# A decode block that records its own instructions and writes its own waits, in place of a scheduling context

## The chip, the cores and the metric

One core of one Trainium2 chip runs the kernel. The metric is device time in microseconds (us) of one execution. The engines are TensorE (PE, its weight loads PEld), VectorE (DVE), ScalarE (ACT), GpSimd (POOL) and SyncE (SP), which here issues every DMA. Each engine works through its own queue of instructions in order; engines and DMAs are tied together by semaphores only.

## What is computed

One decode step for 4 tokens of width 448: layer norm, attention with 16 query heads over 8 heads of cached keys and values (the last 1024 positions of 4096), an output projection with a residual, then two layer norms and a two-layer MLP with a GELU, and a second residual.

```python
def _A_ref(x, k_cache, v_cache, wq, wo):          # B, Sq, D = 4, 1, 448
    Hq, Dh = 16, 256
    Hkv, Sk = k_cache.shape[1], k_cache.shape[2]  # 8, 4096
    W = min(4096, max(256, Sk // 4))              # 1024
    rep = Hq // Hkv
    q = (x @ wq).reshape(B, Sq, Hq, Dh).transpose(0, 2, 1, 3)
    k = jnp.repeat(k_cache[:, :, Sk - W:, :], rep, axis=1)
    v = jnp.repeat(v_cache[:, :, Sk - W:, :], rep, axis=1)
    p = _softmax(jnp.einsum("bhqd,bhkd->bhqk", q, k) * (Dh ** -0.5), axis=-1)
    o = jnp.einsum("bhqk,bhkd->bhqd", p, v)
    return o.transpose(0, 2, 1, 3).reshape(B, Sq, Hq * Dh) @ wo

def _B_ref(x, w1, b1, w2, b2):                    # F = 1792
    y = _layernorm(x, axis=-1)
    h = _gelu(jnp.einsum("bsd,df->bsf", y, w1) + b1)
    return jnp.einsum("bsf,fd->bsd", h, w2) + b2

x = A_x
h = x + _A_ref(_layernorm(x, axis=-1), A_k_cache, A_v_cache, A_wq, A_wo)
h2 = h + _B_ref(_layernorm(h, axis=-1), B_w1, B_b1, B_w2, B_b2)
```

All of it is float32, and nearly all of the bytes are the cached keys and values and the weights, each read once.

## The kernel before

**Loads.** The host lays the inputs out so that each DMA fills 128 partitions with long rows. On the chip a ring of three slots (`slot`, 15872 columns of float32 each) takes them in turn, all issued by SyncE in the order of the program (`load`, line 58, and line 285 for two small ones): `t0` (first query weights and the token, then the first keys), `l1` to `l8` (keys, values and projection weights, 6 or 8 MB each), and last the slots `te0`, `te1` and `te2`, which are filled in pieces: keys `k7`, values with output weights `vo`, values `v7` in two pieces, output weights `wo`, then `w1` in two pieces and `w2` in four. A load into a slot waits until the slot's former contents have been read. Three loads ahead of the computation are thus under way or queued.

**Computation.** The eight heads of keys and values are taken in pairs, each pair giving one tile `n` of 0 to 3. `project` and `queries` make the queries (tile `qT`), `scores` (line 184) multiplies them with the keys, `softmax` (lines 187 to 205) takes the maximum on VectorE and the exponential on ScalarE, `transpose_p` (line 212) turns the probabilities on PE and copies them to `pT` on VectorE (line 218), `values` (line 226) multiplies with the values into `po`, `transposed_output` scales by the reciprocal of the sums (`rec`, lines 203 and 204; line 243) and transposes, and `add_output` (line 257) adds the projection to `acc`. Between tiles PE runs matmuls on a zeroed bfloat16 tile `idle` (`keep_warm`, line 269), whose results nothing reads.

**Head.** While the first loads come, the constants are made: `ident` by GpSimd, `sel` and `fold` from it by VectorE (lines 97 to 114), zeroed tiles by memsets. Then the first layer norm (lines 288 to 296) gives `yT`, and three copies spread token and biases over `wide` (lines 301 to 306). The reciprocal root is a power taken on GpSimd (`rsqrt`, line 148).

**Tail.** After the last values: residual and sums (line 464), two mean subtractions, variances, `w1` (`pu`, line 501), GELU (line 508), then `w2`: its first 8 chunks into `pa` (line 528), which ScalarE copies (`pas`), the other 6 into `py` (line 539) together with `pas`. `hb` (line 482) is the residual with a bias; `res` (line 545) adds it to `py`, and line 546 stores `res`, 64 KB.

**Order and waits.** The body runs inside a scheduling context (`tile.TileContext`, line 619). Tiles come from its pools, it finds which instructions depend on each other, sets the semaphores and waits, and places the tiles. With `manual_schedule` the queues of PE, SP and ACT keep the order of the program; those of VectorE and GpSimd are ordered by the context. At the context's end stand instructions of its own, which carry line 619 in the profile. Those of line 614 are the setup of the program object.

Of the kernel before, what the change touches and what calls it, by code (L numbers as in the profile page):

```python
# [1 line left out]

# [5 lines left out]

F32 = mybir.dt.float32
BF16 = mybir.dt.bfloat16  # L10
AF = mybir.ActivationFunctionType
ALU = mybir.AluOpType
AX = mybir.AxisListType
PSUM = bass.MemoryType.PSUM

B, D = 4, 448
HQ, HKV, SK, DH = 16, 8, 4096, 256
# [3 lines left out]
P = 128  # L21
# [9 lines left out]
SLOT = CACHE + 2 * WEIGHTS + HALF  # L31
# [1 line left out]
EPS = 1e-5  # L33
SCALE = DH ** -0.5

@with_exitstack
def block_kernel(ctx: ExitStack, tc, wq0, k0, wq1, l1, l2, l3, l4, l5, l6, l7, l8, k7, vo, v7, wo, w1, w2, out):
    nc = tc.nc
    const = ctx.enter_context(tc.tile_pool(name="const", bufs=1))
    ring = ctx.enter_context(tc.tile_pool(name="ring", bufs=3))  # L40
    work = ctx.enter_context(tc.tile_pool(name="work", bufs=2))
    once = ctx.enter_context(tc.tile_pool(name="once", bufs=1))
    ps_s = ctx.enter_context(tc.tile_pool(name="ps_s", bufs=2, space=PSUM))
    ps_t = ctx.enter_context(tc.tile_pool(name="ps_t", bufs=2, space=PSUM))
    ps_o = ctx.enter_context(tc.tile_pool(name="ps_o", bufs=1, space=PSUM))
    ps_m = ctx.enter_context(tc.tile_pool(name="ps_m", bufs=2, space=PSUM))
    ps_w = ctx.enter_context(tc.tile_pool(name="ps_w", bufs=1, space=PSUM))

    def slot(name):
        return ring.tile([P, SLOT], F32, tag="r", name=name)

    def load(t, at, src, pieces=None):
        dst = t[:, at : at + src.shape[-1]]
        at = 0
        for n in pieces or (src.shape[-1],):
            nc.sync.dma_start(dst[:, at : at + n], src[:, at : at + n])  # L58
            at += n
        return dst  # L60

    def cut(t, sizes):
        parts, at = [], 0
        for n in sizes:
            parts.append(t[:, at : at + n])
            at += n
        return parts
# [11 lines left out]
    def keys(t):  # L79
        return t.rearrange("p (c b k) -> p c b k", c=2, b=B)  # L80
# [7 lines left out]


    ident = const.tile([P, P], F32, name="ident")  # L90
    make_identity(nc, ident)
    mhalf = const.tile([P, B], F32, name="mhalf")
    nc.vector.memset(mhalf, -0.5)
    mean = const.tile([P, P], F32, name="mean")
# [83 lines left out]
    def score_tiles(n):  # L178
        return [ps_s.tile([P, 512], F32, tag="s", name=f"s{n}_{h}") for h in range(2)]

    def scores(s, g, h, kt):
        for c in range(2):
            for b in range(B):
                nc.tensor.matmul(  # L184
                    s[h][b * Q : (b + 1) * Q, :], qT[g][:, c, b, :], kt[:, c, b, :],
                    start=(g == 0 and c == 0), stop=(g == 1 and c == 1),
                )

    def softmax(n, s):
        mx = work.tile([P, 2], F32, tag="mx", name=f"mx{n}")  # L190
        for h in range(2):
            nc.vector.reduce_max(mx[:, h : h + 1], s[h], axis=AX.X)  # L192
        nm = work.tile([P, 1], F32, tag="nm", name=f"nm{n}")
        nc.vector.tensor_scalar(nm, mx[:, 0:1], mx[:, 1:2], -SCALE, op0=ALU.max, op1=ALU.mult)  # L194
        p = once.tile([P, 2 * 512], F32, tag="p", name=f"p{n}")
        sums = work.tile([P, 2], F32, tag="sums", name=f"sums{n}")
        for h in range(2):
            nc.scalar.activation(  # L198
                p[:, h * 512 : (h + 1) * 512], s[h], AF.Exp, bias=nm, scale=SCALE,
                accum_out=sums[:, h : h + 1],  # L200
            )
        rec = work.tile([P, 1], F32, tag="rec", name=f"rec{n}")
        nc.vector.tensor_add(rec, sums[:, 0:1], sums[:, 1:2])
        nc.vector.reciprocal(rec, rec)
        return p, rec

    def transpose_p(n, p):
        pts = []
        for h in range(2):
            pt = ps_t.tile([P, 4, P], F32, tag="t", name=f"ppt{n}_{h}")  # L210
            for c in range(4):
                nc.tensor.transpose(pt[:, c, :], p[:, (4 * h + c) * P : (4 * h + c + 1) * P], ident)  # L212
            pts.append(pt.rearrange("p (c i) (b q) -> p c i b q", i=2, b=B))
        for g in range(2):
            for h, src in enumerate(pts):
                for i in range(2):
                    at = (2 * g + i) * REP
                    nc.vector.tensor_copy(
                        pT[g][:, 2 * h : 2 * h + 2, :, at : at + REP],
                        src[:, :, i, :, 2 * g * REP : (2 * g + 1) * REP],  # L220
                    )

    def values(g, vt, po, pairs=range(NKC // 2), alone=False):
        for c in pairs:
            for b in range(B):
                nc.tensor.matmul(  # L226
                    po[b * Q : (b + 1) * Q], pT[g][:, c, b, :], vt[c][:, :, b, :],
                    start=(c == 0 and (alone or g == 0)), stop=(c == NKC // 2 - 1 and (alone or g == 1)),
                )
# [5 lines left out]
    def columns(t, j):  # L235
        if j < 3:
            return t[:, j * P : (j + 1) * P].rearrange("p (i c) -> p i c", i=2)
        return t[:, None, 3 * P :].to_broadcast([t.shape[0], 2, H])
# [32 lines left out]
    def keep_warm_between():  # L271
        warm = ps_t.tile([P, 512], F32, tag="t", name="between")
        keep_warm(6, warm)

    def po_tile(g, pool=ps_o, tag="o"):
        return pool.tile([P, 2, DH], F32, tag=tag, name=f"po{g}")


    t = slot("t0")
    wqt, xT, b2T, b1T = cut(load(t, 0, wq0), (WEIGHTS, ND * B, 4, 4 * 4))  # L280
    wqt = wq_parts(yT[0], wqt)
# [25 lines left out]
    for at, n in ((0, 2), (2 * P, 4)):  # L307
# [3 lines left out]
        cols = min(n * P, rs.shape[1] - at)  # L311
# [4 lines left out]
    s = score_tiles(0)  # L316
# [3 lines left out]
    def both_queries(n, wqs):  # L320
        pq = pq_tile(n)
        for g in range(2):
            project(pq, wq_parts(yT[g], wqs[g]), g == 0)
        queries(n, pq)

    def outputs(n, po, rec, wos):
        transposed_output(n, po, rec, range(2))
        for g in range(2):
            add_output(n, g, output_weights(wos[g]))

    ka, kb, va = cut(load(slot("l1"), 0, l1), (HALF, HALF, HALF))
    for h, kt in enumerate((ka, kb)):
        scores(s, 1, h, keys(kt))
    p, rec = softmax(0, s)
    transpose_p(0, p)
    po = po_tile(0)
    values(0, chunks(va), po, range(0, 2))
    keep_warm_between()

    vb, v, wo_a, wo_b = cut(load(slot("l2"), 0, l2), (HALF, CACHE, WEIGHTS, WEIGHTS))  # L340
# [7 lines left out]
    s = score_tiles(1)  # L348
# [4 lines left out]

    k2, v, wq_a, wq_b = cut(load(slot("l4"), 0, l4), (HALF, CACHE, WEIGHTS, WEIGHTS))
    scores(s, 1, 1, keys(k2))
    p, rec = softmax(1, s)
    both_queries(2, (wq_a, wq_b))
    transpose_p(1, p)
    po = po_tile(1)
    values(0, chunks(v), po)  # L360
    keep_warm_between()

    v, wo_a, wo_b, ka = cut(load(slot("l5"), 0, l5), (CACHE, WEIGHTS, WEIGHTS, HALF))
    values(1, chunks(v), po)
    s = score_tiles(2)
# [5 lines left out]
    scores(s, 0, 1, keys(kb))  # L371
    for h, kt in enumerate((ka, k2)):
        scores(s, 1, h, keys(kt))
    p, rec = softmax(2, s)
    transpose_p(2, p)
    keep_warm_between()

    v, va, wq_a, wq_b = cut(load(slot("l7"), 0, l7), (CACHE, HALF, WEIGHTS, WEIGHTS))
# [8 lines left out]
    s = score_tiles(3)  # L387
# [7 lines left out]
    v, wot = cut(load(e[1], 0, vo), (CACHE, 2 * D))  # L395
# [6 lines left out]
    w2t = cut(load(e[2], CACHE, w2, (8 * D, 3 * D, 2 * D, D)), NFC * (D,))  # L402
    for h in range(2):
        scores(s, 1, h, kt[h])
    p, rec = softmax(3, s)


    warm0 = ps_o.tile([P, 512], F32, tag="o", name="warm0")
# [1 line left out]
    def fill(n):  # L410
        for _ in range(n):
            nc.tensor.matmul(warm0[:Q], yT[0][:, 0, :], kt[0][:, 0, 0, :], start=True, stop=True)

    fill(2)
    transpose_p(3, p)
    fill(3)
    po = po_tile(3)
    values(0, vt, po, alone=True)
# [27 lines left out]
    def w1_part(a, j):  # L446
        if a < 3:
            return slice(0, P), w1t[3 if a == 2 else a][:, FQ * j : FQ * (j + 1)]
        rows = slice(H * (j // 2), H * (j // 2) + H)
        return rows, w1t[2][rows, FQ * (j % 2) : FQ * (j % 2 + 1)]  # L450


    def row_mean(sums, at, name):
        nc.tensor.matmul(at, fold, sums, start=True, stop=True)
        return at

    def stat(name):
        return once.tile([P, 1], F32, tag=name, name=name)
# [7 lines left out]
    m = row_mean(hs, pm[:, 0:1], "m")  # L466
# [4 lines left out]
    m = row_mean(ds, pm2[:, 0:1], "m2")  # L471
# [14 lines left out]
    s = stat("r2")  # L486
# [10 lines left out]
    for a in (0, 1, 3, 2):  # L497
        m = Q if a == 0 else B
        for j in range(4):
            rows, w = w1_part(a, j)  # L500
# [23 lines left out]
    first = 8  # L524
    pa = ps_w.tile([P, D], F32, tag="acc", name="pa")
    for c in range(first):
        j, m = c % 4, Q if c < 4 else B
# [6 lines left out]
    for c in range(first, NFC):  # L534
        g = gT[:, c, :] if c < 12 else gT_last[:, c - 12, :]
        for j in range(4):
            m, n = (Q, 2) if c == first else (B, 2 if j < 3 else 1)
            w = columns(w2t[c], j) if n == 2 else w2t[c][:, None, 3 * P :]
# [5 lines left out]
    res = once.tile([P, P], F32, tag="res", name="res")  # L544
    nc.vector.tensor_add(res, py.rearrange("p i c -> p (i c)"), hb)  # L545
    nc.sync.dma_start(out, res)


# [76 lines left out]
```

## Time and profile before

| what | us |
|---|---|
| median of 3 runs (lowest, highest) | 213.28 (213.16, 213.37) |
| span of the profiled execution | 211.7 |
| PE busy | 137.8 |
| VectorE busy | 27.6 |
| ScalarE busy | 14.5 |
| GpSimd busy | 5.0 |

The span goes from the first to the last instruction of the program in one profiled execution; the runs' times also hold what lies around it, 213.28 - 211.7 = 1.58 us by the median. Of the profiled execution only the span is shown, no time of its own. The mean TensorE clock granted was 0.878 of full speed. DMA moved 88.42 MB in all, at a mean of 418 GB/s over the span.

A row of the timeline has the start, the length, the engine, the line, the operation, `out<-in`, and in brackets how long the engine had been idle and what ended that. "SPq" and the other names with a q are an engine's sequencer: issues of DMAs, drains, event semaphores (a wait of its own).

### The profile page before, as it was taken

The numbers are of one execution on the slowest core, as the hardware profiler recorded it, in microseconds if no ns is written. First come the engines' busy times: TensorE is split into PE (matmuls) and PEld (weight loads), VectorE is DVE, ScalarE is ACT, GpSimd is POOL, SyncE is SP. The second block draws the span as 40 slices with busy tenths as digits, with TensorE's granted clock in tenths as the row PEclk, the third lists the DMA queues.
The fourth block names the chain that finished last, engine by engine and source line by source line (L and its number), as shares of the span: only waits on it lengthen the run. The fifth ranks groups of instructions, "written<-read, shape, count | busy, mean of one in ns | idle before, by whom it ended". The sixth has DMA issues, their size and how long they took to land.

```text
span 211.7 us, 2238 instructions
## 1 busy us (share of the span) xinstructions
PE 137.8 (65%) x976; PEld 47.4 (22%) x976; DVE 27.6 (13%) x135; ACT 14.5 (7%) x34; POOL 5.0 (2%) x17
## 2 busy tenths in 40 slices
PE   0467846802960688198469586639807997888984
PEld 0330202300220232033112122102302222324332
DVE  1510103100020011013002003100100131103210
ACT  2010000200000000021000002000100002010311
POOL 5100000000000000000000000000000000000200
PEclk9999999995899569859959969666975999999999
DMA  7999998999999999999999999999989999999991
GB/s 294 426 397 471 446 489 384 399 517 408 408 396 516 408 411 396 528 396 408 396 446 427 474 408 471 432 420 420 480 350 430 470 433 393 432 399 442 427 400 60
DMA packets 3256, 88.42 MB, mean 418 GB/s; under 512 B 368, under 2 KB 624, under 8 KB 1200
## 3 DMA queue, kind: packets, MB, share of 16 engines
q1 hardware_dynamic: 3248, 88.30, 97.0%
q8 instruction: 7, 0.11, 0.2%
q14 instruction: 1, 0.01, 0.0%
HBM read 88.23 MB, written 0.07 MB: 417 GB/s over the span
## 4 chain that ended last, share of the span: by engine, by line
DMA 80%; PE 15%; SPq 2%; DVE 1%; issue 1%
DMA l<-l 64%; DMA te<-w 16%; PE po L226 8%; PE acc L257 2%; PE s L184 2%; SPq L58 2%; PE pot L247 1%; PE pa L528 1%; SPq L285 1%; PE py L539 1%; DVE o L243 0%; DVE oT L252 0%; DVE oT L253 0%; PE py L265 0%; DVE res L545 0%
## 5 line engine op out<-in xcount | busy, mean ns | idle before, releaser
L226 PE MATMUL po<-l,pT 128*32 128x512 f32 x192 | 29.5, 770 | 26.4 <-DMA l<-l 26.3
L184 PE MATMUL s<-l,qT 128*32 128x512 f32 x192 | 26.3, 692 | 12.4 <-DMA l<-l 11.8
L226 PEld LDWEIGHTS po<-l,pT 128*32 128x32 f32 x192 | 6.9, 135 | 45.6 <-issue 26.5
L184 PEld LDWEIGHTS s<-l,qT 128*32 128x32 f32 x192 | 6.5, 126 | 30.2 <-issue 19.6
L153 PE MATMUL pq<-l,yT 128*32 128x512 f32 (+1 forms) x60 | 8.7, 726 | 6.9 <-DMA l<-l 6.9
L198 ACT ACTIVATE p<-s,nm 128x512 f32<-128x512 f32 x8 | 5.4, 682 | 91.9 <-DVE nm L194 91.9
L269 PE MATMUL between<-idle 128*32 128x512 bf16 x42 | 11.5, 415 | 0.0
L192 DVE TENSOR_REDUCE mx<-s 128x1 f32<-128x512 f32 x8 | 5.5, 692 | 45.7 <-PE s L184 45.7
L243 DVE TENSOR_SCALAR o<-po,rec 128x512 f32<-128x512 f32 x5 | 3.8, 751 | 57.3 <-PE po L226 57.3
L226 PE MATMUL po<-te,pT 128*32 128x512 f32 x64 | 7.3, 595 | 1.3 <-DMA te<-vo 1.2
L269 PEld LDWEIGHTS <-idle 128*32 128x32 bf16 x64 | 5.9, 100 | 9.8 <-issue 6.1
L212 PE MATMUL ppt<-ident,p 128*128 128x128 f32 x32 | 5.0, 283 | 4.2 <-ACT p L198 4.2
L169 DVE TENSOR_REDUCE sm<-pqt 128x32 f32<-128x128 f32 x4 | 1.2, 292 | 46.5 <-PE pqt L167 46.5
L153 PE MATMUL pq<-t,yT 128*32 128x512 f32 (+1 forms) x16 | 3.9, 952 | 4.9 <-DVE yT L295 2.9
L269 PE MATMUL warm<-idle 128*32 128x512 bf16 x22 | 6.6, 382 | 0.0
L153 PEld LDWEIGHTS pq<-l,yT 128*32 128x32 f32 x60 | 3.7, 149 | 12.9 <-DMA l<-l 7.4
L163 ACT COPY qs<-pq 128x512 f32<-128x512 f32 x4 | 2.3, 586 | 60.1 <-PE pq L153 60.1
L257 PE MATMUL acc<-l,oT 128*32 128x448 f32 x48 | 5.1, 545 | 1.4 <-DVE oT L253 1.4
L184 PE MATMUL s<-t,qT 128*32 128x512 f32 x32 | 5.4, 836 | 0.7 <-DVE qT L176 0.7
L148 POOL TENSOR_TENSOR r<-ve_r,mhalf 128x1 f32<-128x1 f32 x2 | 1.1, 544 | 188.8 <-DVE ve_r L147 188.8
L167 PE MATMUL pqt<-ident,qs 128*128 128x128 f32 x16 | 3.5, 360 | 2.9 <-ACT qs L163 2.9
L212 PEld LDWEIGHTS ppt<-ident,p 128*128 128x128 f32 x32 | 3.4, 141 | 7.6 <-ACT p L198 7.6
(117 smaller groups left out, 83.1 us busy)
## 6 DMA issues: line engine op xcount, KB each, us to landing
l<-l SPq DMA_DIRECT2D x6, 7936.0 KB, 46.8
l<-l SPq DMA_DIRECT2D x2, 6144.0 KB, 34.2
t<-k SPq DMA_DIRECT2D x1, 4864.0 KB, 15.8
te<-vo SPq DMA_DIRECT2D x1, 4544.0 KB, 29.4
te<-k SPq DMA_DIRECT2D x1, 4096.0 KB, 40.0
te<-v SPq DMA_DIRECT2D x1, 3072.0 KB, 17.9
te<-w SPq DMA_DIRECT2D x1, 2240.0 KB, 27.5
te<-w SPq DMA_DIRECT2D x1, 1792.0 KB
```

What stands on the lines that cost most here:

```text
L58: nc.sync.dma_start(dst[:, at : at + n], src[:, at : at + n])
L153: nc.tensor.matmul(pq[j * Q : (j + 1) * Q, cols], y, w, start=start and cols.start == 0, stop=not start and cols.stop == 512,)
L163: nc.scalar.copy(qs, pq)
L167: nc.tensor.transpose(pt[:, i, :], qs[:, i * P : (i + 1) * P], ident)
L184: nc.tensor.matmul(s[h][b * Q : (b + 1) * Q, :], qT[g][:, c, b, :], kt[:, c, b, :], start=(g == 0 and c == 0), stop=(g == 1 and c == 1),)
L192: nc.vector.reduce_max(mx[:, h : h + 1], s[h], axis=AX.X)
L198: nc.scalar.activation(p[:, h * 512 : (h + 1) * 512], s[h], AF.Exp, bias=nm, scale=SCALE, accum_out=sums[:, h : h + 1],)
L212: nc.tensor.transpose(pt[:, c, :], p[:, (4 * h + c) * P : (4 * h + c + 1) * P], ident)
L226: nc.tensor.matmul(po[b * Q : (b + 1) * Q], pT[g][:, c, b, :], vt[c][:, :, b, :], start=(c == 0 and (alone or g == 0)), stop=(c == NKC // ...
L243: nc.vector.tensor_scalar_mul(o, po, rec)
L257: nc.tensor.matmul(acc[i * Q : (i + 1) * Q, :], oT[g][:, i, :], wt[:, i, :], start=(n == 0 and g == 0), stop=(n == 3 if i < 2 else n == 2 ...
L269: nc.tensor.matmul(warm[:Q], idle[:, :Q], idle, start=True, stop=True)
```

## The change

The scheduling context is taken out. `block_kernel` gets the program object itself, and a class `Machine` stands between: each call on an engine is recorded as an `Op` (engine, outputs, inputs), and nothing is emitted until `nc.emit()` behind the last line. Buffers are allocated once by name; `Pool` hands the same one to three of them round in turn, as many as the context's pools had. `_needs` finds, by columns and groups of 4 partitions in SBUF and by whole banks in PSUM, which earlier operations an operation depends on; `emit` drops those that the engine already knows of through another, and sets the rest as waits: the last of them on the instruction itself, further ones as instructions ahead of it (for the bfloat16 matmuls, all of them ahead). A semaphore per engine is raised only by operations that something waits for; each DMA has its own. PE's operations don't wait for PE's. The last instruction is SyncE's wait for the store.

All engines now keep the order of the program, VectorE and GpSimd too. `make_identity` is written out as its two instructions. The two instructions of `rec` move from the end of `softmax` to the end of `transpose_p`, behind the copies to `pT`.

```diff
+class Op:
+    def __init__(self, engine, emit, outs, ins, own):
+        self.engine, self.emit, self.outs, self.ins, self.own = engine, emit, outs, ins, own
+        self.dma = engine == "SP"
...
+class Machine:
+    def __init__(self, nc):
+        self.nc = nc
+        self.issuer = {"PE": nc.tensor, "DVE": nc.vector, "ACT": nc.scalar, "POOL": nc.gpsimd, "SP": nc.sync}
+        self.tensor, self.vector, self.scalar, self.gpsimd, self.sync = (Engine(self, n) for n in self.issuer)
+        self.memory, self.ops = {}, []
...
+    def _needs(self, i, op):
+        needs = set()
+        for a in op.ins:
+            m = self.memory.get(a.tensor.name)
+            if m is not None:
+                rows, cols = m.part(a)
+                needs.update(np.unique(m.wrote[rows, cols]).tolist())
+        for a in op.outs:
+            m = self.memory.get(a.tensor.name)
+            if m is not None:
+                rows, cols = m.part(a)
+                needs.update(np.unique(m.wrote[rows, cols]).tolist())
+                for engine, read in m.read.items():
+                    if engine != op.engine or op.dma:
+                        needs.update(np.unique(read[rows, cols]).tolist())
...
+    def emit(self):
+        ops = self.ops
+        who = [("DMA", i) if op.dma else op.engine for i, op in enumerate(ops)]
...
+        for i, op in enumerate(ops):
+            clock = dict(seen.get(op.engine, {}))
+            needs = sorted(self._needs(i, op), reverse=True)
+            if op.engine == "PE":
+                needs = [j for j in needs if ops[j].engine != "PE"]
+            taken = []
+            for j in needs:
+                if clock.get(who[j], -1) >= j:
+                    continue
+                taken.append(j)
...
+        for i, op in enumerate(ops):
+            marks = [mark[j] for j in waits[i]]
+            issuer = self.issuer[op.engine]
+            alone = op.own == "matmul" and op.ins[0].dtype == BF16
+            for sem, value in marks if alone else marks[:-1]:
+                issuer.wait_ge(sem, value)
+            done = op.emit()
+            if marks and not alone:
+                done.wait_op(*marks[-1], "sem-ge")
+            if op.dma:
+                mark[i] = (self.nc.alloc_semaphore(f"landed_{i}"), 16)
+                done.then_inc(mark[i][0], 16)
+            elif i in waited:
+                count[op.engine] += 1
+                mark[i] = (counter[op.engine], count[op.engine])
+                done.then_inc(counter[op.engine], 1)
+        self.nc.sync.wait_ge(*mark[len(ops) - 1])
...
-def block_kernel(ctx: ExitStack, tc, wq0, k0, wq1, l1, l2, l3, l4, l5, l6, l7, l8, k7, vo, v7, wo, w1, w2, out):
-    nc = tc.nc
...
+def block_kernel(nc, wq0, k0, wq1, l1, l2, l3, l4, l5, l6, l7, l8, k7, vo, v7, wo, w1, w2, out):
+    real, nc = nc, Machine(nc)
...
+    ring = Pool(rows_of_tag, 3)
+    work = Pool(lambda name, shape, dtype: rows_of_tag("w_" + name, shape, dtype), 2)
+    once = Pool(lambda name, shape, dtype: rows_of_tag("o_" + name, shape, dtype), 1)
+    bank = lambda name, shape, dtype: nc.bank("b_" + name)
+    ps_s, ps_t, ps_m = (Pool(bank, 2) for _ in range(3))
+    ps_o, ps_w = (Pool(bank, 1) for _ in range(2))
...
-    make_identity(nc, ident)
+    nc.gpsimd.memset(ident, 0.0)
+    nc.gpsimd.affine_select(
+        out=ident, in_=ident, compare_op=ALU.not_equal, fill=1.0, base=0, pattern=[[-1, P]], channel_multiplier=1
+    )
...
-        rec = work.tile([P, 1], F32, tag="rec", name=f"rec{n}")
-        nc.vector.tensor_add(rec, sums[:, 0:1], sums[:, 1:2])
-        nc.vector.reciprocal(rec, rec)
-        return p, rec
-
-    def transpose_p(n, p):
+        return p, sums
+
+    def transpose_p(n, p, sums):
...
+        rec = work.tile([P, 1], F32, tag="rec", name=f"rec{n}")
+        nc.vector.tensor_add(rec, sums[:, 0:1], sums[:, 1:2])
+        nc.vector.reciprocal(rec, rec)
+        return rec
...
     nc.sync.dma_start(out, res)
+    nc.emit()
...
-    with tile.TileContext(nc) as tc:
-        with tc.manual_schedule(engines={mybir.EngineType.PE, mybir.EngineType.SP, mybir.EngineType.Activation}):
-            block_kernel(tc, *args, out)
+    block_kernel(nc, *args, out)
```

More of the change, by code (lines that the diff above doesn't have):

```diff
@@ L1 @@
-from contextlib import ExitStack
+import numpy as np
 import concourse.bass as bass
-import concourse.tile as tile
 from concourse import mybir
-from concourse.masks import make_identity
-from concourse._compat import with_exitstack
 F32 = mybir.dt.float32
@@ L13 @@
 AX = mybir.AxisListType
-PSUM = bass.MemoryType.PSUM
 B, D = 4, 448
@@ L34 @@
 SCALE = DH ** -0.5
-@with_exitstack
-def block_kernel(ctx: ExitStack, tc, wq0, k0, wq1, l1, l2, l3, l4, l5, l6, l7, l8, k7, vo, v7, wo, w1, w2, out):
-    nc = tc.nc
[L39 to L47, printed above, removed]
+GRANULE = 4
@@ new lines, with __init__, part @@
+class Memory:
+    def __init__(self, shape, psum):
+        self.psum = psum
+        self.row = 1 if psum else int(np.prod(shape[1:]))
+        self.granules = 1 if psum else -(-shape[0] // GRANULE)
+        self.wrote = np.full((self.granules, self.row), -1)
+        self.read = {}
+    def part(self, ap):
+        if self.psum:
+            return slice(0, 1), np.zeros(1, int)
+        pairs = list(ap.ap)
+        first, at = divmod(ap.offset, self.row)
+        rows = slice(first // GRANULE, -(-(first + pairs[0][1]) // GRANULE))
+        cols = np.zeros(1, int)
+        for step, n in pairs[1:]:
+            cols = (cols[:, None] + step * np.arange(n)).ravel()
+        return rows, np.unique(cols) + at
@@ new lines, with __init__, __getattr__, record @@
+class Op:
+    def __init__(self, engine, emit, outs, ins, own):
+        self.engine, self.emit, self.outs, self.ins, self.own = engine, emit, outs, ins, own
+        self.dma = engine == "SP"
+class Engine:
+    def __init__(self, machine, name):
+        self.machine, self.name = machine, name
+    def __getattr__(self, what):
+        def record(*args, **kwargs):
+            issuer = self.machine.issuer[self.name]
+            values = list(args) + list(kwargs.values())
+            aps = [v for v in values if isinstance(v, bass.AP)]
+            outs = [args[0] if args else kwargs["out"]] + [kwargs[k] for k in ("accum_out",) if k in kwargs]
+            ins = [a for a in aps if not any(a is o for o in outs)]
+            self.machine.add(Op(self.name, lambda: getattr(issuer, what)(*args, **kwargs), outs, ins, what))
+        return record
@@ new lines, with sbuf, bank, add @@
+class Machine:
[4 more added lines that the diff above has]
+        self.memory, self.ops = {}, []
+    def sbuf(self, name, shape, dtype=F32):
+        t = self.nc.alloc_sbuf_tensor(name, list(shape), dtype)
+        self.memory[t.name] = Memory(shape, False)
+        return t[tuple(slice(None) for _ in shape)]
+    def bank(self, name):
+        t = self.nc.alloc_psum_tensor(name, [P, 512], F32)
+        self.memory[t.name] = Memory((P, 512), True)
+        return t[:, :]
+    def add(self, op):
+        self.ops.append(op)
+    def _needs(self, i, op):
[13 more added lines that the diff above has]
+                        needs.update(np.unique(read[rows, cols]).tolist())
+        for a in op.ins:
+            m = self.memory.get(a.tensor.name)
+            if m is not None:
+                rows, cols = m.part(a)
+                read = m.read.setdefault(op.engine, np.full((m.granules, m.row), -1))
+                read[rows, cols] = i
+        for a in op.outs:
+            m = self.memory.get(a.tensor.name)
+            if m is not None:
+                rows, cols = m.part(a)
+                m.wrote[rows, cols] = i
+        needs.discard(-1)
+        return needs
+    def emit(self):
+        ops = self.ops
+        who = [("DMA", i) if op.dma else op.engine for i, op in enumerate(ops)]
+        at_start = [None] * len(ops)
+        seen = {}
+        waits = []
+        for i, op in enumerate(ops):
[8 more added lines that the diff above has]
+                taken.append(j)
+                for key, value in list(at_start[j].items()) + [(who[j], j)]:
+                    clock[key] = max(clock.get(key, -1), value)
+            kept = []
+            for j in taken:
+                others = [k for k in taken if k != j]
+                if not any(who[k] == who[j] and k > j or at_start[k].get(who[j], -1) >= j for k in others):
+                    kept.append(j)
+            waits.append(sorted(kept))
+            at_start[i] = clock
+            seen[op.engine] = clock
+        waited = {j for w in waits for j in w}
+        counter = {n: self.nc.alloc_semaphore(f"done_{n}") for n in self.issuer if n != "SP"}
+        count = dict.fromkeys(counter, 0)
+        mark = {}
+        for i, op in enumerate(ops):
[15 more added lines that the diff above has]
+        self.nc.sync.wait_ge(*mark[len(ops) - 1])
@@ new lines, with __init__, tile @@
+class Pool:
+    def __init__(self, make, n):
+        self.make, self.n, self.made = make, n, {}
+    def tile(self, shape, dtype=F32, tag="", name=""):
+        ring = self.made.setdefault(tag, [[], 0])
+        if len(ring[0]) < self.n:
+            ring[0].append(self.make(f"{tag}_{len(ring[0])}", shape, dtype))
+        t = ring[0][ring[1] % self.n]
+        ring[1] += 1
+        size = int(np.prod(shape[1:]))
+        flat = t[: shape[0], :size]
+        if len(shape) == 2:
+            return flat
+        names = " ".join(f"a{i}" for i in range(len(shape) - 1))
+        return flat.rearrange(f"p ({names}) -> p {names}", **{f"a{i}": n for i, n in enumerate(shape[1:])})
@@ new lines, in block_kernel, with rows_of_tag, flat @@
+def block_kernel(nc, wq0, k0, wq1, l1, l2, l3, l4, l5, l6, l7, l8, k7, vo, v7, wo, w1, w2, out):
+    real, nc = nc, Machine(nc)
+    def rows_of_tag(name, shape, dtype):
+        return nc.sbuf(name, (P, int(np.prod(shape[1:]))), dtype)
+    def flat(name, shape, dtype=F32):
+        t = nc.sbuf(name, (shape[0], int(np.prod(shape[1:]))), dtype)
+        return Pool(lambda *_: t, 1).tile(shape, dtype, "x")
+    class const:
+        tile = staticmethod(lambda shape, dtype, name: flat(name, shape, dtype))
+    ring = Pool(rows_of_tag, 3)
[4 more added lines that the diff above has]
+    ps_o, ps_w = (Pool(bank, 1) for _ in range(2))
@@ L51, in slot @@
     def slot(name):
-        return ring.tile([P, SLOT], F32, tag="r", name=name)
+        return ring.tile([P, SLOT], F32, tag="slot", name=name)
     def load(t, at, src, pieces=None):
@@ L333, in block_kernel @@
         scores(s, 1, h, keys(kt))
-    p, rec = softmax(0, s)
-    transpose_p(0, p)
+    p, sums = softmax(0, s)
+    rec = transpose_p(0, p, sums)
     po = po_tile(0)
@@ L355, in block_kernel @@
     scores(s, 1, 1, keys(k2))
-    p, rec = softmax(1, s)
+    p, sums = softmax(1, s)
     both_queries(2, (wq_a, wq_b))
-    transpose_p(1, p)
+    rec = transpose_p(1, p, sums)
     po = po_tile(1)
@@ L373, in block_kernel @@
         scores(s, 1, h, keys(kt))
-    p, rec = softmax(2, s)
-    transpose_p(2, p)
+    p, sums = softmax(2, s)
+    rec = transpose_p(2, p, sums)
     keep_warm_between()
@@ L404, in block_kernel @@
         scores(s, 1, h, kt[h])
-    p, rec = softmax(3, s)
+    p, sums = softmax(3, s)
     warm0 = ps_o.tile([P, 512], F32, tag="o", name="warm0")
@@ L414, in block_kernel @@
     fill(2)
-    transpose_p(3, p)
+    rec = transpose_p(3, p, sums)
     fill(3)
@@ L546, in block_kernel @@
     nc.sync.dma_start(out, res)
+    nc.emit()
 def kernel(A_x, A_k_cache, A_v_cache, A_wq, A_wo, B_x, B_w1, B_b1, B_w2, B_b2):
-    import numpy as np
     import concourse.bacc as bacc
```

## The prediction, made before the change was run

> **What bounds the kernel now.** I read the page first: the span, the busy shares, the DMA queue's share, the shares of the chain.
>
> ```profile
> span 211.7 us, 2238 instructions
> ...
> PE 137.8 (65%) x976; PEld 47.4 (22%) x976; DVE 27.6 (13%) x135; ACT 14.5 (7%) x34; POOL 5.0 (2%) x17
> ...
> q1 hardware_dynamic: 3248, 88.30, 97.0%
> ...
> DMA 80%; PE 15%; SPq 2%; DVE 1%; issue 1%
> ```
>
> No engine is above 65%. The one queue with the loads is 97.0% of 16 engines' span: 0.97 x 211.7 = 205.4 us. The chain of waits says "DMA 80%, PE 15%", which could be read as if PE were worth a sixth of the time. The table by stage (us, busy time of PE, PEld, DVE, ACT, POOL, then granted clock, DMA share, GB/s) tells whether the queue ever stops while PE stands in the chain.
>
> ```profile
> 60.00:100.00 40.00, 25.27 (x168) 9.15 (x172) 4.27 (x26) 2.62 (x6) 0.00 (x0) 0.79 1.00 434
> 140.00:180.00 40.00, 30.24 (x196) 9.04 (x196) 4.67 (x23) 2.03 (x5) 0.00 (x0) 0.84 0.98 424
> 180.00:200.00 20.00, 17.56 (x171) 7.35 (x171) 4.20 (x16) 2.62 (x6) 0.95 (x2) 1.00 1.00 425
> ```
>
> It doesn't: the DMA share is 0.98 to 1.00 at 424 to 434 GB/s, also where the clock granted to PE is 0.79. So the middle is bytes over rate, 88.30 MB at about 430 GB/s = 205 us, and PE in the chain only marks when a slot of the ring comes free. Whether it comes free in time is read from SyncE's queue, near the end, where the queue is shortest.
>
> ```profile
> 150.85 0.33 SPq L58 DMA_DIRECT2D te<-vo  x1
> 169.75 0.80 SPq L58 DMA_DIRECT2D te<-v  x2
> ...
> 180.25 0.33 SPq L58 DMA_DIRECT2D te<-w  x1
> 187.68 0.33 SPq L58 DMA_DIRECT2D te<-w  x1
> te<-vo SPq DMA_DIRECT2D x1, 4544.0 KB, 29.4
> te<-v SPq DMA_DIRECT2D x1, 3072.0 KB, 17.9
> te<-w SPq DMA_DIRECT2D x1, 448.0 KB, 27.7
> te<-w SPq DMA_DIRECT2D x1, 224.0 KB, 20.8
> SPq L58 <- DMA te<-vo: 7.2, 1, 7.2
> ```
>
> The last rows of a DMA are its size and the time from issue to landing. The load `vo` lands at 150.85 + 29.4 = 180.25; the next, `v7`, is issued at 169.75, when l8's slot comes free. So 10.5 us of bytes were still queued: a slot could come free that much later, or any time earlier, at no cost. The last two pieces of `w2` were issued late, 180.25 and 187.68, each after an older DMA had landed (`vo` at 180.25, for which SyncE waited 7.2 us, and `v7` at 169.75 + 17.9 = 187.65), and still landed in order, at 207.95 and 208.48. After that comes what no load hides:
>
> ```profile
> 172.08 33.21 DMA te<-w
> 205.29 0.14 issue
> 205.43 1.71 PE pa L528 x16
> ...
> 209.02 0.29 DVE res L545
> ```
>
> The first piece of `w2` lands at 205.29, and from there `pa`, `py` and `res` run to 209.31. The store and the end:
>
> ```profile
> 209.34 0.35 SPq L546 DMA_DIRECT2D out<-res  x1
> out<-res SPq DMA_DIRECT2D x1, 64.0 KB, 1.5
> L619 SPq EVENT_SEMAPHORE  x1: 28/28/28, 210.9 to 210.9; - x1
> L619 SPq DRAIN  x3: 7/7/7, 211.0 to 211.3; - x3
> L619 POOLq EVENT_SEMAPHORE_RANGE_CLEAR  x1: 96/96/96, 211.3 to 211.3; - x1
> L619 DVEq EVENT_SEMAPHORE  x2: 21/21/21, 211.2 to 211.7; - x2
> ```
>
> The store lands at 209.34 + 1.5 = 210.84, and SyncE's wait for it (line 619 is the scheduling context's exit) ends about 210.95. Then follow two rounds of all five engines, with drains and a clear of the semaphores by POOL between, to 211.70. So the time has three parts: a head before the stream, a stream of 205 us set by bytes, a tail of 6.4 us.
>
> **The change part by part.** The sum is made against the profiled execution: span 211.70. The runs shown have a median of 213.28, so 1.58 us lie around the span, which I carry over unchanged.
>
> *The exit.* The context's exit goes; the program's last instruction is SyncE's wait for the store. That wait exists already, with its 28 ns; what follows it goes: 211.70 - 210.95 = 0.75 us. The bounds are 0.70 (the first drain of SyncE at 211.0) and 0.86 (the landing at 210.84). I take 0.75. Nothing lies beside these instructions, so all of it counts, if the time outside the span stays.
>
> The Trainium skill, "Runtime: NRT & Kernel Launch", section "The ~15µs preamble/postamble breakdown", says that the runtime puts its own barrier (about 1.5 us) and its own semaphore reset (about 1.5 us) behind every kernel. By that the context's exit is work done twice and all 0.75 us can go; but also the runtime's barrier might already be waiting on the slowest engine's shutdown. The 1.58 us that the runs show around the span are less than the page's two figures together, so not all of that is in this measurement.
>
> *The head.* SyncE's first DMA follows the barrier of the program's setup (line 614), which the new kernel keeps, for that object is still made the same way.
>
> ```profile
> L614 SPq EVENT_SEMAPHORE  x1: 17/17/17, 0.7 to 0.7; - x1
> 0.73 0.38 SPq L58 DMA_DIRECT2D t<-wq  x1
> ...
> 9.27 1.03 POOL L148 TENSOR_TENSOR rx<-ve_x,mhalf 128x4 f32<-128x4 f32 x1 [5.81 <-DVE sel L98]
> ...
> 11.31 0.17 DVE L294 TENSOR_TENSOR yT<-d_x,rx 128x12 f32<-128x12 f32 x1
> 17.04 0.20 PEld L153 LDWEIGHTS pq<-t,yT 128*32 128x32 f32 x6 [2.41 <-DMA t<-k]
> ```
>
> Nothing precedes the first load, so the stream starts at the same time: 0. VectorE and GpSimd, which the context ordered itself, now go in program order. `sel`, `fold` and the memsets come ahead of the first wait for data and the three `wide` copies come behind `yT`. The reciprocal root ends at 10.30 and `yT` came only at 11.31, so `yT` is about 1 us earlier. It buys nothing: PE waits at 17.04 for the DMA of `k0`. If the load were no cover, the gain would be 1 us.
>
> *The stream.* The order of loads, their sizes and the queue stay. The waits before a load are now by columns read, not by whole tiles, so `v7` may be issued 1 or 2 us earlier; and with a semaphore for each DMA, `w2`'s last pieces are issued with the rest at about 174. Both only lengthen a queue that wasn't empty: 0. Queued behind SyncE's waiting loads is only the store, at 209. The bounds are in the rows by stage: between 424 and 434 GB/s for all 88.30 MB lie 208.3 and 203.5 us, so 4.8 us by rates that this one execution shows; but the three runs lie within 0.21 us of each other, so the mean rate is far steadier than that. I take 0 and allow 0.2.
>
> The Trainium skill, "DMA: Bandwidth & Descriptors", section "Where 436 GB/s comes from", gives 435 GB/s as the ceiling of the SBUF ports and about 358 as what HBM allows a core, and says that the latter binds for loads. The trace disagrees with the lower figure (424 to 434) and sits at the higher one. By the higher one the stream can't be faster than an estimated 88.30 / 0.435 = 203 us, so finer waits can't find much there.
>
> *The tail and the recorded waits.* `hb` moves behind `zT`, and the two instructions of `rec` behind the copies of `pT`.
>
> ```profile
> 195.24 0.29 DVE L482 TENSOR_TENSOR hb<-h,rs 128x128 f32<-128x128 f32 x1
> 197.38 0.17 DVE L480 COPY zT<-pz 128x16 f32<-128x16 f32 x1 [0.57 <-PE pz L479]
> 198.23 0.16 DVE L147 TENSOR_SCALAR ve_r<-pv 128x1 f32<-128x1 f32 x1 [0.68 <-PE pv L454]
> L203 DVE TENSOR_TENSOR rec<-sums x4: 149/150/159, 38.3 to 175.9; 128x1 f32<-128x1 f32 x4
> 58.16 0.75 DVE L243 TENSOR_SCALAR o<-po,rec 128x512 f32<-128x512 f32 x1 [18.87 <-PE po L226]
> L528 PEldq EVENT_SEMAPHORE  x1: 51/51/51, 205.3 to 205.3; - x1
> ```
>
> `hb` fits into the 0.68 us in which VectorE waits for `pv` (197.55 + 0.29 = 197.84). `rec` isn't wanted until `o`, before which VectorE is idle 18.87 us in the first tile. Without the cover they cost 0.29 and 2 x 0.15 = 0.30. As to the waits: one that needs a single semaphore rides on its instruction, only further ones are instructions, and one such on PE takes 51 ns. Between 205.3 and 209.3 seven instructions wait (five of PE, `res`, the store); one more each would be at most 7 x 0.05 = 0.35 us, one fewer where PE has one now is -0.05. I take 0, since the old kernel has the same dependencies.
>
> *Sum.* 211.70 - 0.75 + 0 + 0 + 0 = 210.95, plus 1.58: **212.5 us**, 0.35% less. With -0.86 and 0.70, the stream's 0.2 either way and the waits' -0.05 to +0.35, this case reaches from 212.2 to 213.1; most of it is below 212.85.
>
> **The rivals.**
>
> *The exit only changes its place*: the program's build puts an end of its own there, or what comes after the span waits for the same thing, and the 1.58 us grow by the 0.75. Then the time is 213.28. For it: the time around the span isn't shown by any row. Against it: the rows at the end all carry line 619, the context's own.
>
> *More goes than the span shows*: PE, ACT, POOL and DVE no longer wait for SyncE, and shut down while the store is under way. The two rounds took 211.0 to 211.7, 0.35 us each. If the 1.58 us hold one such round, 212.53 - 0.35 = 212.2; the bound, all of it gone, is 211.0. Nothing shows it.
>
> *Slower, by one mechanism*: the queue shares its rate among DMAs that are queued together. With `w2`'s last pieces (448 + 224 KB) issued at 174 rather than at 180 and 187, `w2`'s first piece would land later by up to 0.69 MB / 0.43 = 1.6 us, and `pa` with it: 213.28 + 1.6 - 0.75 = 214.1. It decides from 0.75 + 0.43 = 1.18 us on, where the loss is over 0.2%. Against it: the pieces that were queued together landed in order of issue, and a 10 us queue never let a later one pass.
>
> **How the numbers follow.** A measurement of this kernel can tell about 0.2%, 0.43 us, from no change. Chances: forecast 0.60, more goes 0.10, the exit only moves 0.20, slower 0.10. Faster is then 0.70, the same 0.20, slower 0.10 (what of the forecast's case lies above 212.85 is matched by partial moves of the exit that still lie below it). The range reaches from 212.1, below the case with one round gone, to 213.4, which takes in the exit that only moves; slower and the far end of more, about 0.15, are left out. The sign doesn't hang on the range's middle, for the likeliest case has its own, 212.2 to 213.1.
>
> **What would show it.** Right: no group of line 619 and no rows of any engine behind SyncE's wait for `out<-res`, with the span ending about 0.1 us after the store's landing; SyncE's first DMA still at 0.73; the queue's share times span still about 205 us; the first piece of `w2` landing at 205.3 within 0.2; all of `w2` issued by 175; `yT` about 1 us earlier with the wait for `k0` longer by as much. Wrong: drains and event semaphores at the end; a span shorter by 0.75 with an unchanged time (what is around it grew); `w2`'s first piece landing a microsecond later while its last lands at 208.5 as before (shared rate); a stage of the stream under 0.97 of DMA share (a wait of the new kernel that frees a slot more than 10 us late).

## The result and the profile after

| kernel | median us | runs | ratio to before, 95% interval |
|---|---|---|---|
| before | 213.25 | 4 | |
| after | 212.06 | 4 | 0.9942 [0.9928, 0.9956] |

The change takes 1.19 us off, 0.6%: faster, as forecast, but by 1.6 times the 0.75 us forecast, and 0.04 us below the range. Of the run called exit_back below, the profiled execution was a disturbed one (314.97 us), so its times and spans are read from its other ten, and none of its rows.

In the new kernel each instruction is emitted by the recorder, so nearly all rows carry line 74, and one tells them apart by the buffers' names: `b_acc`, `b_o`, `b_m` and `b_s` are banks of PSUM, `slot` the ring, `o_res` is `res`. The page of after:

```profile
span 210.7 us, 2189 instructions
...
q1 hardware_dynamic: 3248, 88.30, 97.5%
...
DMA 78%; PE 17%; SPq 2%; DVE 1%; issue 1%; ACT 0%
```

The queue's share times the span, 0.975 x 210.7 = 205.4 us, is what it was before (205.4). The rates by stage of after (the columns as before):

```profile
60.00:100.00 40.00, 23.92 (x176) 9.04 (x180) 4.54 (x27) 2.51 (x6) 0.00 (x0) 0.83 1.00 432
140.00:180.00 40.00, 30.27 (x196) 9.20 (x196) 4.72 (x23) 2.03 (x5) 0.00 (x0) 0.81 0.98 425
180.00:200.00 20.00, 17.44 (x170) 7.36 (x171) 4.10 (x16) 2.62 (x6) 0.83 (x2) 1.00 1.00 424
```

424 to 432 GB/s against 424 to 434: the stream is the same stream. The timeline of SyncE in after, and the only row that stands behind the store (line 177 is SyncE's wait for it):

```profile
0.74 0.39 SPq L74 DMA_DIRECT2D slot<-wq  x1
...
147.50 0.33 SPq L74 DMA_DIRECT2D slot<-vo  x1
168.93 0.80 SPq L74 DMA_DIRECT2D slot<-v  x2
169.77 0.43 SPq L74 DMA_DIRECT2D slot<-wo  x1
170.25 9.82 SPq L74 DMA_DIRECT2D slot<-w  x6
209.13 0.35 SPq L74 DMA_DIRECT2D out<-o_res  x1
```

```profile
L177 SPq EVENT_SEMAPHORE  x1: 17/17/17, 210.7 to 210.7; - x1
```

The first load goes out at 0.74, as before (0.73). Behind the store there is one wait, and with it the span ends: no drain, no round of the five engines. From the issue of the store to the end it is 210.7 - 209.13 = 1.57 us, where it was 211.7 - 209.34 = 2.36. That is 0.79 of the 1.19 us. The store itself went out 0.21 earlier in this pair of profiled executions, which the experiments had to explain, and so had the rest: what lies around the span was 1.58 us by the arithmetic of the prediction and is now 212.03 - 210.7 = 1.33 by the profiled run's own time.

### The profile page after: what moved, and what is told of

Read it like the earlier page. It is cut to its first block, busy times and chain, and to the rows that moved or that the text cites. A ratio compares the mean times of both kernels' runs of the same rounds, so it can differ in the third digit from the quotient of the medians.

```text
span 210.7 us, 2189 instructions
## 1 busy us (share of the span) xinstructions
PE 138.5 (66%) x976; PEld 47.2 (22%) x976; DVE 28.8 (14%) x135; ACT 14.4 (7%) x34; POOL 5.0 (2%) x17
## 4 chain that ended last, share of the span: by engine, by line
DMA 78%; PE 17%; SPq 2%; DVE 1%; issue 1%; ACT 0%
DMA slot<-l 64%; DMA slot<-w 14%; PE b_o L74 9%; PE b_s L74 4%; PE b_acc L74 3%; SPq L74 2%; PE b_m L74 1%; DVE oT L74 1%; DVE w_o L74 0%; PE b_t L74 0%; DVE o_u L74 0%; ACT o_u L74 0%; DVE o_res L74 0%
## 5 line engine op out<-in xcount | busy, mean ns | idle before, releaser
L74 PE MATMUL b_o<-slot,pT 128*32 128x512 f32 x224 | 32.3, 729 | 26.3 <-DMA slot<-l 25.6
L74 PE MATMUL b_s<-slot,qT 128*32 128x512 f32 x256 | 38.7, 760 | 14.3 <-DMA slot<-l 12.9
L74 PE MATMUL b_m<-slot,yT 128*32 128x512 f32 (+1 forms) x76 | 11.4, 705 | 11.4 <-DMA slot<-l 6.2
L74 PEld LDWEIGHTS b_s<-slot,qT 128*32 128x32 f32 x256 | 9.4, 136 | 40.8 <-issue 23.9
L74 PEld LDWEIGHTS b_o<-slot,pT 128*32 128x32 f32 x224 | 7.7, 130 | 47.5 <-DMA slot<-l 28.0
L74 PE MATMUL b_t<-idle 128*32 128x512 bf16 x64 | 17.7, 397 | 0.5 <-DVE pT L74 0.5
L74 DVE TENSOR_REDUCE w_mx<-b_s 128x1 f32<-128x512 f32 x8 | 5.5, 691 | 49.5 <-PE b_s L74 49.5
L74 ACT ACTIVATE o_p<-b_s,w_nm 128x512 f32<-128x512 f32 x8 | 5.4, 682 | 96.4 <-DVE w_nm L74 96.4
L74 PEld LDWEIGHTS b_t<-idle 128*32 128x32 bf16 x64 | 5.9, 99 | 9.9 <-issue 5.2
L74 PE MATMUL b_acc<-slot,oT 128*32 128x448 f32 x52 | 6.1, 546 | 1.9 <-DVE oT L74 1.9
## 6 DMA issues: line engine op xcount, KB each, us to landing
slot<-vo SPq DMA_DIRECT2D x1, 4544.0 KB, 32.9
```

What stands on the lines that cost most here:

```text
L74: self.machine.add(Op(self.name, lambda: getattr(issuer, what)(*args, **kwargs), outs, ins, what))
```

## The experiments

All but the last are the new kernel or the old one with a single thing put back, taken out or moved. The table gives for each the median time, the median span, and the mean over its runs of time minus span, which is the measure that settles the case. The kernel before ran beside each group.

| kernel | runs | us | span | time minus span |
|---|---|---|---|---|
| before (beside exit_back, before_noexit, late_issue, all_wait) | 17 | 213.27 | 211.5 | 1.77 |
| before (beside the four only_ kernels) | 7 | 213.37 | 211.6 | 1.78 |
| before (beside early_loads) | 7 | 213.22 | 211.4 | 1.79 |
| after | 4 | 212.06 | 210.7 | 1.33 |
| exit_back | 10 | 213.34 | 211.55 | 1.80 |
| before_noexit | 5 | 212.10 | 210.8 | 1.34 |
| late_issue | 5 | 211.98 | 210.6 | 1.32 |
| all_wait | 7 | 212.60 | 210.8 | 1.84 |
| only_dve | 4 | 212.07 | 210.65 | 1.42 |
| only_act | 4 | 212.16 | 210.65 | 1.50 |
| only_pe | 4 | 212.30 | 210.7 | 1.58 |
| only_pool | 4 | 212.54 | 210.7 | 1.84 |
| early_loads | 4 | 211.35 | 210.05 | 1.32 |

### The exit alone, put back and taken out

```diff
...
     nc.emit()
+    real.all_engine_barrier()
+    real.clear_and_free_semaphores(nc.sems)
+    real.all_engine_barrier()
```

> The new kernel with the old exit put back behind its last instruction: drain and barrier of all five engines, clear of the semaphores by GpSimd, barrier again. Theory A (the exit is what both the span and the time around it lost, 0.79 + 0.22 us): 212.06 + 1.0 = 213.1 us, span 211.5, time around the span 1.55. Rival B (the 0.22 around the span came from something else, the branches or the shorter program): 212.85 us, span 211.5, around it 1.33. Rival C (the exit is free and the gain came from the stream): 212.1.

Measured: 213.34 us, ratio to before 1.0007 [0.9998, 1.0016]; span 211.55, around it 1.80. Theory A holds: with its exit the new kernel takes the old one's time, to 0.07 us. Rival C falls, and so does B, for the time around the span came back too.

```diff
             block_kernel(tc, *args, out)
+    end = nc.main_func.blocks[-1]
+    end.instructions = list(end.instructions)[:1]
     r = run(nc, [arrays], core_ids=[0])
```

> The old kernel, scheduling context and all, with its exit cut down to SyncE's first drain, which waits for the store. Theory A: 213.25 - 0.79 - 0.22 = 212.24 us, span 210.9, store still at 209.34. Rival B (only the span's part goes): 212.46 us. Rival C (the exit's time only moves out of the span): 213.25 us with a span of 210.9.

Measured: 212.10 us, ratio 0.9945 [0.9932, 0.9959], against 0.9942 for the whole change. The rows of line 619 that are left in it:

```profile
L619 SPq EVENT_SEMAPHORE  x5: 27/28/28, 210.0 to 211.1; - x5
L619 SPq DRAIN  x1: 13/13/13, 211.2 to 211.2; - x1
```

SyncE's waits for what is outstanding and one drain. Theory A again, to 0.14 us. The two runs together say that the recorder, the finer waits, the order of VectorE and the fixed buffers together come to nothing that can be measured: 213.34 against 213.27 with the exit, 212.06 against 212.10 without. They also speak to the 0.21 us by which the store went out earlier. In the profiled run of before_noexit, which has the old stream, the store goes out later still:

```profile
209.57 0.35 SPq L546 DMA_DIRECT2D out<-res  x1
```

But that run took 212.53 us where the kernel's median is 212.10. Executions of one kernel differ by some tenths (the 17 spans of before go from 211.3 to 211.7), so 0.21 us between two of them needs no cause in the kernel.

### The late pieces of `w2`

Before, SyncE issued the last two pieces of `w2` at 180 and 188; after, it turned to them right behind the rest, at 172.25 and 172.73, though the issue of the last one then took until 180.07 (see the last section). This was the most visible change in the stream, so the 0.21 us was tried on it.

```diff
...
+            if op.dma and op.ins[0].tensor.name == "w2":
+                pieces.append(i)
+                if len(pieces) > 2:
+                    needs.add(next(j for j, o in enumerate(ops) if o.dma and o.ins[0].tensor.name == ("vo", "v7")[len(pieces) - 3]))
...
```

> The new kernel, but SyncE issues the last two pieces of w2 as late as before: one after vo has landed (180), one after v7's first piece (188). Theory D (the 0.2 us by which w2 landed earlier come from the early issue): w2's first piece lands at 205.3, store at 209.3, 212.27 us. Rival E (they come from something else in the program): 212.06 us, store at 209.1.

Measured: 211.98 us, span 210.6. In its profile the pieces are late again and the store is not:

```profile
169.53 18.36 SPq L74 DMA_DIRECT2D slot<-w  x6
209.00 0.35 SPq L74 DMA_DIRECT2D out<-o_res  x1
```

Theory D falls. With 17 runs of the kernel before beside it, whose median span is 211.5 and not 211.7, the 0.21 us is most likely the profiled execution of before, which was 0.2 us longer than its kernel's median.

### What lies around the span

exit_back and before_noexit put 0.43 to 0.47 us of the gain outside the span, where no row is. The old exit releases all five engines last; the new end lets four of them stop early. So the other four were made to wait for the store too:

```diff
-        self.nc.sync.wait_ge(*mark[len(ops) - 1])
+        for n in ("SP", "PE", "DVE", "ACT", "POOL"):
+            self.issuer[n].wait_ge(*mark[len(ops) - 1])
```

> The new kernel, but PE, VectorE, ScalarE and GpSimd also wait for the store before they end. Theory A (the 0.22 us around the span are those engines' shutdown, which the old exit held back until the end): span 210.7 to 210.8, 212.25 us. Rival B (the 0.22 belongs to the barrier's rounds themselves or to the branches): 212.06 us, within 0.1.

Measured: 212.60 us, ratio to before 0.9971 [0.996, 0.9982]. The span hardly moves, and nothing is added to it but four waits beside SyncE's:

```profile
L178 SPq EVENT_SEMAPHORE  x1: 17/17/17, 210.7 to 210.7; - x1
L178 ACTq EVENT_SEMAPHORE  x1: 17/17/17, 210.7 to 210.7; - x1
L178 POOLq EVENT_SEMAPHORE  x1: 17/17/17, 210.7 to 210.7; - x1
L178 DVEq EVENT_SEMAPHORE  x1: 21/21/21, 210.7 to 210.7; - x1
L178 PEldq EVENT_SEMAPHORE  x1: 51/51/51, 210.7 to 210.7; - x1
```

Yet the time is 0.54 us longer, 0.5 of it in time minus span, which is back at 1.84. Theory A had the sign and half of the size (0.2), because it went by the wrong 1.55. Which of the four it is, or whether it is five ending at once, four kernels tell, in each of which a single engine has the last wait:

```diff
-        self.nc.sync.wait_ge(*mark[len(ops) - 1])
+        self.issuer["POOL"].wait_ge(*mark[len(ops) - 1])
```

> The new kernel, but the last wait, for the store, is PE's; SyncE ends when it has issued the store. Span about 210.75 in all of these. Theory F (each engine needs a time of its own after its last instruction, and the latest sets the measured time; with SyncE last it is 1.33 us, with all five 1.8, so one of the other four needs 1.8): between 212.1 and 212.6 us, PE's is the likeliest to be the long one, 212.55. Rival G (the 0.46 us come from five engines ending at once, none needs more than SyncE): 212.1 us, as for the other three.

> The same with ScalarE as the one that waits for the store. Theory F: 210.75 plus ScalarE's own time, 212.1 to 212.55. Rival G: 212.1 us, as for the others.

> The same with VectorE as the one that waits for the store. Theory F: 210.75 plus VectorE's own time, 212.1 to 212.55. Rival G: 212.1 us, as for the others.

> The same with GpSimd as the one that waits for the store. Theory F: 210.75 plus GpSimd's own time, 212.1 to 212.55; if it is under SyncE's 1.33, under 212.0. Rival G: 212.1 us, as for the others.

In each of the four, line 177 is one row, of the engine named; in only_pool:

```profile
L177 POOLq EVENT_SEMAPHORE  x1: 17/17/17, 210.6 to 210.6; - x1
```

Measured, as time minus span: VectorE 1.42, ScalarE 1.50, PE 1.58, GpSimd 1.84, SyncE 1.33 (after). Theory F holds and G falls: the time from the last wait to the end of the measurement depends on the engine that waits last. The guess that PE's is the long one was wrong; it is GpSimd's, and GpSimd alone gives the 1.84 of all five together. What an engine does in that time, and whether it is work of its own or its place in an order common to all, no trace here shows.

### The other end

If the time is a head, a stream set by bytes and a tail, the barrier of the program's setup at 0.73 costs in the same way as the exit did, for SyncE waits in it with nothing under way. Six loads that wait for nothing were moved ahead of SyncE's wait for that barrier, behind its own report to it:

```diff
     block_kernel(nc, *args, out)
+    block = nc.main_func.blocks[0]
+    todo = list(block.instructions)
+    sp = [i for i in todo if i.engine == mybir.EngineType.SP]
+    release = next(i for i in sp if i.opcode == "EventSemaphore")
+    first = [i for i in sp if i.opcode == "DMACopy"][:6]
+    moved = {i.name for i in first}
+    rest = [i for i in todo if i.name not in moved]
+    at = [i.name for i in rest].index(release.name)
+    block.instructions = rest[:at] + first + rest[at:]
```

> The new kernel, but SyncE issues its first six loads (wq0, k0, the two of wq1, l1, l2) before it waits for the barrier of the program's setup, after it has reported to that barrier. Theory H (the time is a head, then a stream set by bytes, then a tail, and the barrier at the start costs in the same way as the one at the end): first DMA at about 0.05 in place of 0.74, all landings 0.7 earlier, span 210.0, 211.4 us. Rival I (the tail's engines or something in the stream hold the end where it is): first DMA at 0.05, store still at 209.1, 212.06 us.

Measured: 211.35 us, ratio to before 0.9907 [0.9891, 0.9924], 0.71 us less than after.

```profile
0.09 0.39 SPq L74 DMA_DIRECT2D slot<-wq  x1
...
208.34 0.35 SPq L74 DMA_DIRECT2D out<-o_res  x1
```

The first load goes out 0.65 us earlier (0.09 for 0.74), the store 0.79 (208.34 for 209.13), and the median span is 0.65 shorter. Theory H holds and I falls: what the head gives, the stream carries through to the end. This is the fastest version of all that ran.

## Why the prediction was wrong, step by step

**What bounds the kernel: right.** The stream is 205.4 us before and after; late_issue, with its different times of issue, leaves the end alone, and early_loads moves it by what the head gave.

**The exit: right in mechanism and size, as far as the span goes.** Forecast 0.75 within 0.70 to 0.86; the rows give 0.79 from the store's issue to the end of the span, and exit_back against after gives a span longer by 0.85.

**"1.58 us lie around the span, which I carry over unchanged": this step failed**, and twice. The 1.58 was the median of some runs less the span of one other execution. Each run's own time less its own span is 1.77 before, over 17 runs. That slip alone moved no forecast, since span and 1.58 add up to the median either way. But the term isn't unchanged: it is 1.33 after, and the 0.44 us that went with it is the term that the sum put at nothing. The runs put it down to GpSimd, behind whose last wait 1.84 us follow, where 1.33 follow SyncE's. The old exit keeps GpSimd to the end:

```profile
L619 POOLq EVENT_SEMAPHORE  x4: 17/17/17, 211.0 to 211.6; - x4
```

That is about 0.1 us ahead of the end of the span, and 1.84 - 0.1 is an estimate of 1.74 for what lies around it, near the 1.77. The new end has no such wait, and GpSimd's last operation ends at 200.26 (199.72 + 0.54). 0.79 + 0.44 = 1.23, against 1.19 measured.

The rival "more goes than the span shows" had this mechanism, engines that shut down while the store is under way, at 0.35 us and a chance of 0.10. Its size was near (0.44), by luck: the 0.35 was the length of one round of the exit, and what went is the difference between two engines' ends. It was given too little because no row shows it; but no row showed the opposite either, and the range's lower end, 212.1, lay only 0.1 below this rival's own 212.2.

The Trainium skill, "Runtime: NRT & Kernel Launch", section "The ~15µs preamble/postamble breakdown", puts a barrier and a reset of semaphores by each engine behind the kernel. That each engine still has something to do after its last instruction fits the runs (1.33 to 1.84 us, by the engine that ends last). The page gives one figure for the reset and none by engine; the differences measured here, 0.51 us from SyncE to GpSimd, aren't in it.

**The head: right.** `yT` is 1.4 us earlier (a forecast of 1), and PE waits that much longer for `k0`:

```profile
9.91 0.43 DVE L74 TENSOR_TENSOR yT<-w_d,w_rx 128x12 f32<-128x12 f32 x3 [1.15 <-POOL w_rx L74]
16.97 0.20 PEld L74 LDWEIGHTS b_m<-slot,yT 128*32 128x32 f32 x6 [3.78 <-DMA slot<-k]
```

The weight load's wait for `k0` goes from 2.41 to 3.78 us, and takes up all of the gain.

**The tail and the waits: right.** `hb` and `rec` fell into the gaps that were named for them:

```profile
197.60 0.28 DVE L74 TENSOR_TENSOR o_hb<-o_h,rs 128x128 f32<-128x128 f32 x1
198.35 0.16 DVE L74 TENSOR_SCALAR w_ve<-b_m 128x1 f32<-128x1 f32 x1 [0.47 <-PE b_m L74]
41.02 0.16 DVE L74 RECIPROCAL w_rec<-w_rec 128x1 f32<-128x1 f32 x1
59.24 0.75 DVE L74 TENSOR_SCALAR w_o<-b_o,w_rec 128x512 f32<-128x512 f32 x1 [18.05 <-PE b_o L74]
```

VectorE still waits 0.47 us for PE behind `hb`, and 18.05 us behind `rec`. What the recorded waits cost can't be told apart from the other changes in the middle; all of them together are the 0.04 us between before_noexit and after, which is within the noise.

**The slower rival didn't occur, as far as it was put to the test.** Two of the signs named for the stream missed: the last piece of `w2` was not issued by 175 (its issue ended at 180.07), and the first piece landed 0.24 us from the 205.29 of before, where 0.2 was allowed, but early. The first and the last piece in after (the last number is the time from issue to landing, the issues at 171.25 and 172.73):

```profile
slot<-w SPq DMA_DIRECT2D x1, 1792.0 KB, 33.8
...
slot<-w SPq DMA_DIRECT2D x1, 224.0 KB, 35.6
```

They land at 205.05 and 208.33, the first of them not a microsecond late. In late_issue, which has the last two pieces late again, the chain shows the first piece's landing at the end of this row, 204.95:

```profile
170.52 34.43 DMA slot<-w
```

So the piece of 448 KB that was issued 8 us earlier (172.25 for 180.30) went with a landing that differs by 0.1 us, where the rival's arithmetic for its 0.46 MB at 0.43 MB per us gives 1.1. The last piece, held until 180.07, tests the rival less.

## What to carry to other kernels

Where the middle of a kernel is bytes over rate, look at its two ends: here the exit's rounds were worth 0.8 us, the engine that stops last 0.5, and the barrier ahead of the first load 0.7, while a new set of waits and orders in the middle was worth nothing. Let the engine with the shortest end of its own be the last one, let the others stop early, and issue loads that wait for nothing ahead of a barrier that they don't need. The old exit also clears the semaphores, which the new end leaves out; whether anything else needs that clear, no run here shows. And compare each run's time with its own span: a median less another execution's span hides a difference of some tenths.

## What the runs showed of the hardware that was not expected

The time from the last wait to the end of the measurement depends on the engine that waits: SyncE 1.33 us, VectorE 1.42, ScalarE 1.50, PE 1.58, GpSimd 1.84.

SyncE can be held up in issuing a DMA whose wait is already over. In after, the last piece of `w2` waits for matmuls on l8's keys, which had ended by 171.1, and its issue took 7.34 us instead of 0.4:

```profile
172.73 7.34 SPq L74 DMA_DIRECT2D slot<-w  x1
```

Nine DMAs were outstanding at that time (`vo`, two of `v7`, `wo`, two of `w1`, three of `w2`), and the issue ended at 180.07, when the oldest, `vo`, was about to land (147.50 + 32.9 = 180.4). In the six other runs that issue this piece as early it took 6.93 to 7.63 us, and ended about 0.3 us ahead of the landing of `vo` each time. It costs nothing here, since SyncE has only the store left to issue. That the outstanding DMAs hold it is inferred from these times; whether DMAs, their pieces or their bytes are counted stays open.
